# A fused attention and cosine-gated MLP kernel: the order of all engines and the sharing of copies and squares chosen anew

## The chip, the cores and the metric

The kernel runs on one core of one Trainium2 chip. The core has a matrix engine (TensorE, in the profile PE, with its weight loads as PEld), a vector engine (VectorE, DVE), an activation engine (ScalarE, ACT), a general engine (GpSimd, POOL) and a queue engine for transfers (SyncE, SP). The metric is device time in microseconds (us) of one execution, lower is better. The engines run side by side and wait for each other through semaphores.

## The reference

```python
q_n = q / (norm(q) + 1e-06); k_n = k / (norm(k) + 1e-06)      # 8 x 12 heads, 448 x 64
scores = q_n @ k_n.T / 0.1
attn = softmax(scores)                                          # over the last axis
x = (attn @ v), heads side by side                              # 3584 x 768
h = x @ w_in                                                    # 768 x 2048
out = (h * cos(h)) @ w_out                                      # 2048 x 768, float32
```

So there is cosine attention for 8 batches of 12 heads, and a gated two-layer MLP on all 3,584 tokens.

## The kernel before, in words

**Tiling.** Two heads make a "group" (48 groups, numbered g), three groups a "unit" (16 units u, half of a batch), six groups a batch b. For a unit, k and q are loaded (`load`), squared (`square`, label sq), summed over 64 columns (`reduce`, red), turned into reciprocal norms (`rnorm`) and scaled (`scale`). A scaled group is transposed (label T, or TP for the first nine, which TensorE transposes), and TensorE computes its scores in four pieces SC g.0 to SC g.3, where piece 0 is half as wide. ScalarE turns each piece into exponentials (exp g.c). From those TensorE forms the weighted values and the sums (`attend`: steps R, AV, S). VectorE can add exponentials in pairs first ("folds": fold g; "tails": tail g), so that TensorE has fewer sums to form: a group with two folds needs two matmul steps fewer than one with one fold, and a tail saves one R step.

**Normalising.** For groups that are not in the list `direct`, the unnormalised result is copied out of PSUM (label xu, by ScalarE if g is in the list `acts`, otherwise by VectorE, lines 1114 to 1117). Per unit, `chain` (line 1182) collects the sums by a transfer, takes reciprocals, writes them to memory and broadcasts them back into RB (labels gather, recip, spread, bcast). `multiply` (line 1170) then forms x g, on VectorE if g is in the list `fast`, otherwise on GpSimd. Both are line 1175.

**MLP.** For each batch b, M1 b.n computes sixteen blocks of 128 features (6 matmuls each over 448 tokens, line 1209), in eight pairs; ScalarE takes the cosine (sin, line 1240) and VectorE the product (g, line 1242). M1 b needs x of all six groups of its batch; `m1` in the plan says how many pairs begin with a part of the groups, from which group on they go singly, in which PSUM bank each pair stands, and in which order the groups are taken. M2 t computes 128 output rows (28 tiles t): as quarter-size matmuls (line 1309) or, from tile 21 on, as full ones (line 1338). A tile's two halves are copied out of PSUM by ScalarE if (t, half) is in `oacts` (line 1274) and otherwise by VectorE (line 1276), and stored.

**Order.** TensorE's order is written out in the plan ("order", some 1,450 entries, a label and a count each), and so is the bank of each step ("script"). The other engines' orders come from a planner in the kernel's own code (class `Program`, `arrange` and `play`, lines 367 to 563): it plays the program through with assumed costs, and at each moment lets an engine take, among what is ready, the operation with the earliest due time. The due time is counted back from TensorE's order, plus a number of its own for each operation (`bias`, some 1,000 numbers). The planner also plays the instruction packets of TensorE: 256 instructions each, where `ins` is the number of instructions that an operation holds. The result is a fixed program: each engine has a list of instructions in order and waits on semaphores. SyncE's list holds the loads, transposes, gathers, broadcasts and stores; GpSimd issues the loads of v and of the weights.

**Dummies.** At the start, while data is awaited, TensorE runs dummy matmuls on a zeroed buffer (line 1375).

Of the kernel before, what the change touches and what calls it, by code (L numbers as in the profile page):

```python
# [1595 lines left out]
```

## Time and profile before

| What | us |
|---|---|
| median of 3 runs | 419.7 |
| lowest, highest | 419.03, 424.96 |
| profiled execution, its own time | 419.64 |
| its span, first to last instruction | 417.7 |
| TensorE busy | 405.9 |
| ScalarE busy | 289.1 |
| VectorE busy | 242.6 |
| GpSimd busy | 217.8 |

The span is what the trace covers; 1.9 us of the execution's time lie around it. Busy time of TensorE is the union of its matmuls' records; consecutive matmuls overlap in the records, so the duration of one is longer than the time that it adds. In a row of groups stand the line, the engine, the operation, the output and inputs, the shape and the count, then busy time and mean duration in nanoseconds, then the idle time before them and what ended it. In rows in order of time the first number is the start, the second the length, and the bracket tells of idle time before and who ended it.

### The profile page before, as it was taken

The page shows a single profiled execution, that of the slowest core. Times are in us where ns is not written, and L with a number is a line of the kernel's source. Part 1 is how long each engine was busy: PE and PEld are TensorE (multiplying, and loading weights), DVE is VectorE, ACT ScalarE, POOL GpSimd, SP SyncE. Part 2 cuts the span into 40 slices and gives each one's busy share as a digit, 9 for nine tenths or more (in the row PEclk, how much of TensorE's full clock was granted, in tenths as well). Part 3 has the DMA queues.
Part 4 walks back from the last instruction along what each step waited for, and adds up shares of the span by engine and source line. Part 5 has one row for each costly group of instructions (what it writes and reads, how often), then busy time and mean ns, then how long its engine had stood idle before and what let it go on. Part 6 is the DMA issues. An engine that isn't in the chain of part 4 may idle for free.

```text
span 417.7 us, 14563 instructions
## 1 busy us (share of the span) xinstructions
PE 405.9 (97%) x6511; PEld 255.7 (61%) x6511; DVE 242.6 (58%) x321; ACT 289.1 (69%) x403; POOL 217.8 (52%) x173
## 2 busy tenths in 40 slices
...
PEclk9999999999999999999999999999999999999999
...
GB/s 190 251 258 221 206 213 182 173 151 197 197 118 146 170 236 186 101 140 219 236 92 87 192 269 83 137 198 215 206 81 96 186 3 3 105 123 2 5 72 113
DMA packets 77352, 63.31 MB, mean 152 GB/s; under 512 B 42090, under 2 KB 72298, under 8 KB 77290
## 3 DMA queue, kind: packets, MB, share of 16 engines
...
q0 software_dynamic: 18048, 12.59, 20.3%
q8 instruction: 51, 0.84, 0.8%
...
q10 hardware_dynamic: 160, 0.10, 0.1%
...
## 4 chain that ended last, share of the span: by engine, by line
PE 85%; ACT 4%; DVE 4%; DMA 3%; POOL 2%; issue 1%; SPq 0%; DVEq 0%; ACTq 0%; POOLq 0%
PE MP L1309 22%; PE SC L1209 21%; PE AV L1209 10%; PE MP L1338 5%; PE SC L975 5%; PE AV L1057 4%; PE MP L1209 4%; PE SC L1057 4%; PE SC L1338 3%; DMA RB<-scr 1%; ACT PX L989 1%; DMA scr<-rcp 1%; PE AV L975 1%; POOL qks L918 1%; PE SC L982 1%
## 5 line engine op out<-in xcount | busy, mean ns | idle before, releaser
L1309 PE MATMUL MP<-W,gT 64*64 64x384 bf16 x2688 | 137.3, 323 | 0.5 <-DVE qkT L956 0.4
L989 ACT ACTIVATE PX<-SC 128x896 bf16<-128x896 f32 x116 | 103.3, 917 | 13.5 <-PE SC L975 10.9
L1209 PE MATMUL SC<-xT,W 128*128 128x448 bf16 x468 | 96.9, 353 | 0.0
L1309 PEld LDWEIGHTS MP<-W,gT 64*64 64x64 bf16 x2688 | 80.9, 107 | 24.3 <-issue 2.3
L918 POOL TENSOR_TENSOR qks<-raw,rn 128x896 bf16<-128x896 f32 (+1 forms) x45 | 75.2, 1681 | 31.7 <-ACT rn L910 14.2
L1175 POOL TENSOR_TENSOR xT<-xu,RB 128x448 bf16<-128x448 f32 x39 | 44.4, 1151 | 84.4 <-DMA RB<-scr 42.9
L1209 PEld LDWEIGHTS SC<-xT,W 128*128 128x128 bf16 x468 | 45.4, 98 | 43.2 <-issue 1.5
L1240 ACT ACTIVATE cosb<-SC,cst 128x896 f32<-128x896 f32 x39 | 39.1, 1007 | 45.1 <-PE SC L1209 41.3
L1242 DVE TENSOR_TENSOR gT<-SC,cosb 128x896 bf16<-128x896 f32 x39 | 42.3, 1090 | 42.1 <-ACT cosb L1240 40.7
L887 DVE TENSOR_REDUCE n<-sq 128x14 f32<-128x896 bf16 (+2 forms) x49 | 51.0, 1057 | 12.4 <-ACT sq L878 8.8
L880 POOL TENSOR_TENSOR sq<-raw 128x896 bf16<-128x896 f32 x31 | 52.0, 1693 | 11.0 <-DVE n L887 5.8
L993 DVE TENSOR_TENSOR FO<-PX 128x896 bf16<-128x896 bf16 x37 | 30.0, 811 | 32.6 <-ACT PX L989 32.4
L1209 PE MATMUL AV<-xT,W 128*128 128x448 bf16 x216 | 48.1, 353 | 0.0
L975 PE MATMUL SC<-qkT 64*64 64x448 bf16 x464 | 42.4, 354 | 0.8 <-ACT PH L989 0.3
L854 POOL DMA_DIRECT2D va<-in_v_dram x32 | 21.9, 692 | 22.8 <-PE AV L1057 10.2
L1209 PEld LDWEIGHTS AV<-xT,W 128*128 128x128 bf16 x216 | 20.7, 98 | 19.6 <-issue 0.9
L1276 DVE COPY osb<-MP 128x384 f32<-128x384 f32 x38 | 20.1, 553 | 21.2 <-PE MP L1309 12.3
L989 ACT ACTIVATE PX<-AV 128x896 bf16<-128x896 f32 x28 | 25.7, 917 | 3.9 <-PE AV L975 3.8
L1240 ACT ACTIVATE cosb<-AV,cst 128x896 f32<-128x896 f32 x18 | 18.1, 1006 | 14.9 <-PE AV L1209 12.1
L1338 PE MATMUL MP<-W,gT 128*128 128x384 bf16 x128 | 24.9, 326 | 0.0
L1057 PE MATMUL AV<-PX,va 64*64 64x224 bf16 x480 | 23.1, 258 | 1.7 <-issue 1.3
L1242 DVE TENSOR_TENSOR gT<-AV,cosb 128x896 bf16<-128x896 f32 x18 | 19.6, 1087 | 8.6 <-ACT cosb L1240 7.1
...
## 6 DMA issues: line engine op xcount, KB each, us to landing
...
W<-in_moe_w_out_dram POOLq DMA_DIRECT2D x4, 768.0 KB, 19.3
...
```

The costliest lines, as they stand in the source:

```text
L880: pool(lambda e, x=x, y=y: e.tensor_tensor(y, x, x, ALU.mult), src_, dst, 0.1 + n * 1.78e-3, label="sq%d.%d" % (u, p)).pad = LATE if u > 1 ...
L887: dve(lambda e, w=w: e.tensor_reduce(out=n2v[i][:, 2 * p : 2 * p + 2, w], in_=sqv[p][:, :, w, :], axis=mybir.AxisListType.X, op=ALU.add), ...
L918: f = lambda e, s0=s0, s1=s1: e.tensor_tensor(qksv[i][:, p, s0:s1].rearrange("p s h d -> p h s d"), rawv[i][:, h, s0:s1, :], bass.AP(rn[i] ...
L975: m = e.matmul(ph[BP * o : BP * o + BP, a, 0:S], t[r, c - 1 + (NT3 + 1) * o, 0:BP], x, start=True, stop=True)
L989: act(lambda e: e.activation(PHv[g % 3] if c == 0 else PXv[j][:, c - 1], ph[:, :, 0:n], ACT.Exp, scale=1.0 / TAU), keys, [("PX", j, c) if ...
L1057: m = e.matmul(av_[64 * a : 64 * a + 64, b, x], w, source(kind, c)[r, a, SH * h : SH * h + SH], start=(h == 0 and c == 0 and kind == "V" a ...
L1175: f = lambda e: e.tensor_tensor(x, a, r, ALU.mult)
L1209: t = e.matmul(ph[:, a, 0:S], W1v[:, order[c], 128 * n : 128 * n + 128], xTv[b % 2][:, order[c], :], start=(c == 0), stop=(c == NKC - 1))
L1240: act(lambda e, ph=ph, cz=cz: e.activation(cosv[cz], ph[:, :, 0:S], ACT.Sin, bias=cst.ap()[:, 0:1], scale=1.0), names(gi) + ["cst0"], [("c ...
L1242: dve(lambda e, ph=ph, cz=cz, gi=gi: e.tensor_tensor(gTv[:, 2 * gi : 2 * gi + 2, S * (b % 2) : S * (b % 2) + S], ph[:, :, 0:S], cosv[cz], ...
L1309: r = e.matmul(POH[b][x : x + 64, 0:HW], gTv[k, y, col + x : col + x + 64], W2v[k, y, HW * b : HW * b + HW], start=(y == 0 and h == 0), st ...
L1338: r = e.matmul(po[:, 0 : w[1] - w[0]], gTv[:, y, col : col + 128], W2v[:, y, w[0] : w[1]], start=(y == 0), stop=(y == NF - 1))
```

## The change

Only lists in the plan change, and one number that the planner uses. The functions stay as they are.

- `acts`: which groups' results ScalarE copies out of PSUM.
- `oacts`: which output halves ScalarE copies; 17 before, 24 after.
- `folds`, `tails`: group 16 has two folds in place of one; 13 and 27 get a tail, 30 and 47 lose it; the entries for 8, 9 and 25 belong to groups without folds.
- `squared`, `scaled`: which squares of q and k ScalarE takes (14 before, 12 after; the rest GpSimd), and which three scalings VectorE takes.
- `fast`: which x VectorE multiplies; 3 before, 8 after.
- `m1` for batches 3, 4 and 5; `made`, `flat`.
- `order`, `script` and `bias`: nearly every line is new.
- `ins` of the step B (the spread of reciprocals in the first batch) is 8 in place of 4.

```diff
-    "acts": (7, 8, 9, 17, 18, 19, 22, 24, 25, 26, 28, 29, 30, 34, 35, 37, 40, 42, 43, 44, 47),
-    "oacts": ((0, 0), (4, 0), (5, 0), (10, 0), (12, 0), (13, 0), (14, 0), (16, 0), (16, 1), (21, 0), (22, 1), (23,
-        1), (25, 0), (25, 1), (26, 0), (26, 1), (27, 0)),
-    "made": {1: 4, 2: 8, 3: 11, 4: 13, 5: 27, 6: 20, 8: 21},
+    "acts": (10, 11, 18, 19, 22, 23, 26, 28, 29, 30, 34, 36, 37, 40, 43, 44, 45, 46, 47),
+    "oacts": ((0, 0), (2, 1), (4, 0), (5, 0), (6, 1), (9, 1), (10, 0), (13, 0), (14, 0), (16, 0), (16, 1), (18, 0),
+        (19, 1), (20, 0), (21, 1), (22, 0), (23, 0), (23, 1), (24, 0), (25, 0), (26, 0), (26, 1), (27, 0), (27, 1)),
+    "made": {1: 5, 2: 7, 3: 12, 4: 13, 5: 25, 6: 20, 8: 21},
     "fold": 2,
-    "folds": {6: 2, 7: 0, 8: 0, 9: 0, 10: 1, 11: 1, 12: 2, 13: 1, 14: 1, 15: 1, 16: 1, 17: 0, 18: 1, 21: 1, 25: 0},
+    "folds": {6: 2, 7: 0, 8: 0, 9: 0, 10: 1, 11: 1, 12: 2, 13: 1, 14: 1, 15: 1, 16: 2, 17: 0, 18: 1, 21: 1, 25: 0},
     "tailed": 1,
-    "tails": {6: 0, 7: 0, 8: 1, 9: 1, 10: 0, 11: 0, 12: 0, 13: 0, 14: 0, 15: 0, 16: 0, 17: 0, 18: 1, 21: 0, 27: 0,
-        28: 0, 33: 0, 35: 1, 39: 1, 40: 0, 42: 0, 43: 0},
+    "tails": {6: 0, 7: 0, 8: 0, 9: 0, 10: 0, 11: 0, 12: 0, 13: 1, 14: 0, 15: 0, 16: 0, 17: 0, 18: 1, 21: 0, 25: 0,
+        27: 1, 28: 0, 30: 0, 33: 0, 35: 1, 39: 1, 40: 0, 42: 0, 43: 0, 47: 0},
...
-    "scaled": {(2, 0): "D", (13, 1): "D", (15, 2): "D"},
-    "squared": {(3, 1): "A", (4, 1): "A", (5, 2): "A", (10, 0): "A", (10, 1): "A", (10, 2): "A", (11, 0): "A", (11,
-        1): "A", (12, 2): "A", (13, 0): "A", (13, 1): "A", (13, 2): "A", (14, 0): "A", (15, 1): "A"},
+    "scaled": {(3, 1): "D", (6, 1): "D", (15, 2): "D"},
+    "squared": {(3, 1): "A", (5, 2): "A", (8, 1): "A", (9, 0): "A", (9, 2): "A", (10, 0): "A", (10, 1): "A", (10,
+        2): "A", (11, 1): "A", (13, 0): "A", (15, 0): "A", (15, 1): "A"},
...
-        1, 4)), 3: (3, 2, (0, 2, 1, 0, 2, 1, 0, 2), (0, 1, 2, 5, 3, 4)), 4: (3, 2, (1, 0, 2, 3, 1, 0, 2, 1), (2, 1,
-        0, 3, 4, 5)), 5: (3, 5, (2, 1, 0, 3, 2, 1, 0, 2), (0, 1, 2, 3, 5, 4)), 6: (3, 3, (1, 0, 2, 3, 1, 0, 2, 1),
+        1, 4)), 3: (3, 2, (0, 2, 1, 0, 2, 1, 0, 2), (2, 5, 1, 0, 3, 4)), 4: (4, 2, (1, 0, 2, 3, 1, 0, 2, 1), (2, 1,
+        0, 3, 4, 5)), 5: (4, 5, (2, 1, 0, 3, 2, 1, 0, 2), (0, 1, 2, 3, 5, 4)), 6: (3, 3, (1, 0, 2, 3, 1, 0, 2, 1),
...
-    "flat": (),
-    "fast": (27, 33, 42),
+    "flat": (21,),
+    "fast": (21, 27, 30, 33, 34, 39, 42, 45),
...
-            w = P.op("PE", spread, ["sel0", "sel1", ("gT", 1, NF // 2 - 1), ("RB", i, p)], ["PO"], cost=0.76, mode="F", label="B%d" % g, ins=4)
+            w = P.op("PE", spread, ["sel0", "sel1", ("gT", 1, NF // 2 - 1), ("RB", i, p)], ["PO"], cost=0.76, mode="F", label="B%d" % g, ins=8)
```

The first line of the TensorE order, before and after, as a sample of the rest:

```diff
-        TP0*2 SC0.0 SC0.1 TP1 SC0.2 TP1 SC0.3 SC1.1 SC1.0 TP2 SC1.2 TP2 R0*2 SC2.0 AV0 S0*3 SC1.3 TP3*2 AV0*2 SC2.1 SC2.2
+        TP0*2 SC0.1 SC0.3 SC0.0 TP1*2 SC0.2 SC1.1 SC1.0 TP2*2 SC1.2 R0*2 AV0 S0*2 SC1.3 AV0*2 SC2.0 TP3 S0 SC2.1 SC2.2
...
```

The new order and biases were picked by playing the plan through with lateness drawn at random for transfers and instruction packets.

More of the change, by code (lines that the diff above doesn't have):

```diff
@@ new lines @@
+        TP0*2 SC0.1 SC0.3 SC0.0 TP1*2 SC0.2 SC1.1 SC1.0 TP2*2 SC1.2 R0*2 AV0 S0*2 SC1.3 AV0*2 SC2.0 TP3 S0 SC2.1 SC2.2
+        TP3 R1*2 AV1*2 S1*2 AV1 S1 B0 SC2.3 SC3.0 R2*2 S2 AV2 S2 AV2*2 S2 SC3.1 SC3.2 B1 SC3.3 R3 TP4*2 R3 AV3*3 S3*3
+        SC4.0 SC4.1 B2 R4 SC4.2 TP5*2 SC4.3 B3 SC5.0 R4 SC5.1 AV4 S4*3 AV4*2 SC5.2 SC5.3 M1_0.0 M1_0.1 M1_0.0 R5 M1_0.2
+        R5 AV5 S5*2 AV5*2 S5 M1_0.3 M1_0.4 M1_0.5 M1_0.1 M1_0.0 M1_0.4 M1_0.1 M1_0.6 M1_0.5 M1_0.2 M1_0.3 M1_0.7 M1_0.8
+        M1_0.9 M1_0.10 M1_0.12 M1_0.13 TP6*2 M1_0.11 M1_0.14 TP7*2 M1_0.15 TP8*2 SC6.0 SC6.1 M2_0*4 SC6.2 M2_0 R6*2 AV6
@@ new lines @@
+        SC6.3 SC7.0 M2_0*3 AV6*2 SC7.2 AV6 SC7.1 M2_0*2 SC8.0 AV6*4 SC7.3 M2_0*2 SC8.2 M2_0*2 SC8.1 M2_0 R7*2 AV7 M2_0
+        AV7*6 SC8.3 AV7 M2_1 AV7*3 M2_1*2 AV7 SC9.0 M2_1 SC9.1 M2_1*3 AV8*6 R8*2 SC9.3 SC9.2 AV8*5 M2_1 SC10.1 AV8 M2_1*3
+        SC10.0 M2_1*3 SC10.2 M2_1*2 SC10.3 R9*2 AV9*6 SC11.0 AV9*4 SC11.1 AV9*2 M2_2*3 SC11.2 SC11.3 M2_2*4 R10*2 AV10
+        M2_2 AV10*4 M2_2 SC12.0 AV10*5 M2_2*3 SC12.1 M2_2*4 AV11*5 R11*2 SC12.2 SC12.3 AV11*5 M1_1.0 M1_1.1 M1_1.2 M1_1.3
+        M1_1.2 M1_1.6 M1_1.7 M1_1.6 M1_1.7 M1_1.0 M1_1.1 M1_1.0 M1_1.1 M1_1.0 M1_1.6 M1_1.7 M1_1.6 M1_1.3 M1_1.2 M1_1.3
@@ new lines @@
+        M1_1.2 M1_1.3 M1_1.7 M1_1.6 M1_1.7 M1_1.2 M1_1.3 M1_1.1 M1_1.4 M1_1.0 M1_1.1 M1_1.5 M1_1.4 M1_1.5 M1_1.4 M1_1.5
+        M1_1.4 M1_1.5 M1_1.4 M1_1.5 M1_1.8 M1_1.9 M1_1.12 M1_1.13 M1_1.10 M1_1.11 M1_1.14 M1_1.15 R12*2 AV12*4 SC13.0
+        AV12*3 M2_3*3 AV12 SC13.1 M2_3*2 SC13.2 M2_3 SC13.3 M2_3*2 R13 AV13 M2_3 SC14.0 M2_3 AV13*4 SC14.1 AV13*3 SC14.2
+        AV13*2 M2_3*2 SC14.3 M2_3*2 SC15.0 M2_3*2 SC15.1 R14*2 AV14*5 SC15.2 AV14*5 SC15.3 M2_4*2 SC16.0 M2_4*2 R15
+        SC16.1 R15 M2_4 AV15 SC16.2 M2_4 AV15*4 SC16.3 M2_4 AV15*3 SC17.0 AV15*2 M2_4 SC17.1 M2_4*2 SC17.2 M2_4 AV16
@@ new lines @@
+        SC17.3 AV16*3 R16*2 M2_4 AV16*4 M2_4 SC18.0 M2_4*3 AV17 SC18.1 AV17*5 R17*2 SC18.2 M2_5 AV17 M2_5 AV17 SC18.3
+        AV17*4 R18 M2_5*2 SC19.0 AV18 M2_5*4 SC19.2 M2_5 SC19.1 M2_5 AV18*2 M2_5*2 SC20.0 M2_5*4 AV18*2 SC20.1 AV18*5
+        M2_6 SC19.3 M2_6*7 R19 AV19 SC20.3 M2_6 AV19*2 SC20.2 AV19 M2_6*2 SC21.1 AV19*3 M2_6 AV20*2 AV19 M2_6*2 SC21.2
+        M2_6 SC21.0 AV20*2 R20 M2_6 AV20*3 SC21.3 AV20 M1_2.2 M1_2.3 M1_2.2 M1_2.6 M1_2.7 M1_2.0 M1_2.3 M1_2.2 M1_2.3
+        M1_2.2 M1_2.3 M1_2.2 M1_2.4 M1_2.1 M1_2.0 M1_2.6 M1_2.7 M1_2.1 M1_2.0 M1_2.1 M1_2.0 M1_2.3 M1_2.6 M1_2.7 M1_2.5
@@ new lines @@
+        M1_2.4 M1_2.5 M1_2.4 M1_2.5 M1_2.1 M1_2.0 M1_2.1 M1_2.6 M1_2.4 M1_2.7 M1_2.6 M1_2.7 M1_2.5 M1_2.4 M1_2.5 M1_2.8
+        M1_2.9 M1_2.10 M1_2.11 M1_2.12 M1_2.14 M1_2.13 M1_2.15 M2_7*3 AV21*3 M2_7*2 AV21*2 R21*2 SC22.1 M2_7*2 AV21*3
+        SC22.0 AV21*2 M2_7 SC22.2 M2_7*2 SC22.3 M2_7 SC23.0 M2_7*3 SC23.1 M2_7*2 SC23.2 AV22*4 R22 SC23.3 AV22*4 M2_8*4
+        SC24.1 SC24.0 R23 AV23*2 M2_8*3 SC24.2 AV23 M2_8 AV23 SC24.3 M2_8 AV23*4 M2_8*2 SC25.1 M2_8*5 AV24*2 SC25.0
+        AV24*2 R24 SC25.3 AV24*4 SC25.2 M2_9*4 SC26.0 SC26.1 SC26.2 M2_9*4 AV25 SC26.3 M2_9 AV25*4 SC27.0 AV25 R25*2 M2_9
@@ new lines @@
+        AV25*2 AV26 M2_9*2 AV25*4 AV26*3 R26 SC27.1 M2_9 AV26*4 M2_9*3 SC27.3 SC27.2 M1_3.0 M1_3.1 M1_3.0 M1_3.1 M1_3.0
+        M1_3.1 M1_3.0 M1_3.2 M1_3.3 M1_3.2 M1_3.1 M1_3.0 M1_3.1 M1_3.3 M1_3.2 M1_3.4 M1_3.5 M1_3.4 M1_3.5 M1_3.4 M1_3.5
+        M1_3.3 M1_3.2 M1_3.3 M1_3.2 M1_3.4 M1_3.5 M1_3.4 M1_3.3 M1_3.5 M1_3.6 M1_3.7 M1_3.8 M1_3.9 M1_3.10 M1_3.11
+        M1_3.12 M1_3.13 M1_3.14 M1_3.15 M2_10 R27 M2_10 AV27*4 M2_10 AV27*4 M2_10 SC28.0 SC28.1 M2_10*3 SC28.3 M2_10
+        SC28.2 M2_10*2 SC29.2 SC29.0 M2_10*2 SC29.1 M2_10*4 AV28*4 R28 SC29.3 SC30.0 R28 M2_11*2 AV28*4 R29 AV29*3 M2_11
@@ new lines @@
+        SC30.1 M2_11 AV29 SC30.2 AV29*4 M2_11*4 SC30.3 M2_11*4 SC31.1 M2_11*4 AV30*3 SC31.0 AV30 R30*2 SC31.2 AV30*4
+        SC31.3 M2_12*4 SC32.1 M2_12 SC32.0 M2_12*2 SC32.2 AV31*3 M2_12 AV31 R31 M2_12 AV31*4 SC32.3 SC33.1 M2_12*5 SC33.0
+        M2_12*2 SC33.2 SC33.3 M1_4.0 M1_4.1 M1_4.0 M1_4.1 M1_4.2 M1_4.3 M1_4.6 M1_4.4 M1_4.5 M1_4.4 M1_4.5 M1_4.2 M1_4.3
+        M1_4.4 M1_4.0 M1_4.5 M1_4.2 M1_4.3 M1_4.2 M1_4.3 M1_4.4 M1_4.1 M1_4.0 M1_4.1 M1_4.5 M1_4.0 M1_4.1 M1_4.4 M1_4.5
+        M1_4.2 M1_4.3 M1_4.7 M1_4.6 M1_4.7 M1_4.6 M1_4.7 M1_4.6 M1_4.7 M1_4.6 M1_4.7 M1_4.8 M1_4.10 M1_4.9 M1_4.11
@@ new lines @@
+        M1_4.12 M1_4.13 M1_4.14 M1_4.15 R32 AV32*3 R33 AV32 R33 AV33 AV32 AV33 AV32*3 AV33*2 M2_13 AV33*4 M2_13*3 SC34.0
+        M2_13 SC34.1 M2_13*3 SC34.2 M2_13 SC34.3 M2_13*5 SC35.1 M2_13*2 R34 AV34*2 SC35.0 AV34*2 SC35.3 AV34*4 M2_14*6
+        SC36.0 SC35.2 M2_14*2 SC36.1 M2_14*5 SC36.3 M2_14 AV35*3 M2_14*2 AV35 R35 SC37.2 SC36.2 AV35*4 M2_15*4 SC37.0
+        M2_15*4 SC37.1 M2_15 SC37.3 M2_15*2 R36 AV36*4 M2_15 AV36*4 M2_15*4 AV37 SC38.0 AV37*3 R37 SC38.2 AV37*4 SC38.1
+        M2_16*5 SC38.3 M2_16*3 SC39.1 SC39.0 M2_16*3 SC39.2 M2_16 R38 AV38 M2_16*3 AV38*3 M2_16 SC39.3 AV38*4 M1_5.0
@@ new lines @@
+        M1_5.1 M1_5.0 M1_5.1 M1_5.2 M1_5.3 M1_5.2 M1_5.3 M1_5.4 M1_5.5 M1_5.4 M1_5.6 M1_5.8 M1_5.9 M1_5.5 M1_5.7 M1_5.6
+        M1_5.7 M1_5.10 M1_5.11 M1_5.12 M1_5.13 M1_5.14 M1_5.15 M2_17*2 R39 AV39*3 M2_17 AV39 M2_17 AV39*4 SC40.0 M2_17*2
+        SC40.1 M2_17*2 SC40.2 M2_17 SC41.0 M2_17*2 SC40.3 M2_17 SC41.1 M2_17*2 SC41.2 M2_17*2 SC41.3 R40*2 AV40*4 SC42.0
+        AV40*3 M2_18 AV40 M2_18*2 R41 AV41 SC42.1 AV41*3 SC42.2 AV41*4 M2_18 SC42.3 M2_18*3 SC43.0 AV42 M2_18 SC43.1 AV42
+        M2_18*2 SC43.2 M2_18 SC43.3 AV42*2 M2_18*2 R42*2 AV43 M2_18 AV43 SC44.0 M2_18*2 AV43*2 R43*2 AV42*4 SC44.1
@@ new lines @@
+        M2_19*4 SC44.3 M2_19*2 SC44.2 AV43*4 M2_19*2 SC45.2 M2_19 SC45.0 M2_19*5 SC45.1 SC45.3 M2_19*2 M1_6.2 M1_6.4
+        M1_6.5 M1_6.0 M1_6.3 M1_6.1 M1_6.4 M1_6.2 M1_6.3 M1_6.0 M1_6.1 M1_6.5 M1_6.4 M1_6.2 M1_6.3 M1_6.5 M1_6.0 M1_6.1
+        M1_6.4 M1_6.0 M1_6.1 M1_6.5 M1_6.6 M1_6.7 M1_6.2 M1_6.3 M1_6.8 M1_6.9 M1_6.12 M1_6.10 M1_6.13 M1_6.11 M1_6.14
+        M1_6.15 M2_20 AV45*3 AV44*4 R44 AV45 R45 AV44*2 M2_20 AV44*2 M2_20 SC46.0 AV45*4 M2_20*3 SC46.2 M2_20*2 SC46.1
+        SC46.3 M2_20 SC47.1 M2_20*4 AV46*2 M2_20*3 SC47.0 AV46*2 R46 SC47.3 AV46*4 SC47.2 M2_22*5 M2_21*2 M2_22*2 M2_21*2
@@ new lines @@
+        R47*2 AV47*8 M2_21*6 M2_22 M2_21*6 M2_22*4 M2_23*5 M2_22*4 M2_23*2 M1_7.0 M1_7.1 M1_7.2 M1_7.3 M1_7.0 M1_7.1
+        M1_7.2 M1_7.3 M2_23 M1_7.2 M1_7.4 M1_7.5 M1_7.4 M1_7.3 M1_7.2 M1_7.3 M1_7.2 M1_7.5 M1_7.4 M1_7.3 M1_7.5 M1_7.4
+        M1_7.0 M1_7.1 M1_7.0 M1_7.1 M1_7.5 M1_7.0 M1_7.1 M2_23*2 M1_7.4 M1_7.5 M1_7.8 M2_23 M2_24*2 M1_7.6 M1_7.7 M1_7.10
+        M1_7.11 M2_23*2 M1_7.12 M1_7.9 M2_25 M2_23*3 M1_7.13 M2_24*3 M1_7.14 M1_7.15 M2_24*3 M2_25 M2_24 M2_26 M2_24*2
+        M2_26*4 M2_25*3 M2_26 M2_24*5 M2_25*2 M2_26*2 M2_27*2 M2_26 M2_27 M2_26*2 M2_27 M2_26 M2_25*8 M2_26 M2_25 M2_26*3
@@ L267 @@
+        M2_27*20
         """,
     "script": """
-        s6.0=2 s6.1=1 s6.2=2 s6.3=1 a6=0 s7.0=2 s7.1=1 d6=0 c6=0 s7.2=2 s7.3=1 s8.0=2 d7=0 s8.1=1 a7=0 s8.2=2 s8.3=2 c7=0
-        s9.0=2 d8=0 s9.1=1 s9.2=2 a8=0 s9.3=1 c8=0 s10.0=2 s10.1=1 s10.2=2 a9=0 d9=0 c9=0 s10.3=1 s11.0=2 a10=0 s11.1=1
-        s11.2=2 s11.3=1 d10=0 c10=0 s12.0=2 s12.1=1 d11=0 a11=0 s12.2=2 s12.3=1 c11=0 m1 a12=0 s13.0=2 s13.1=1 d12=0
-        c12=0 s13.2=2 a13=0 s13.3=1 s14.0=2 s14.1=1 d13=0 c13=0 s14.2=2 a14=0 s14.3=1 s15.0=2 s15.1=1 s15.2=2 d14=0 c14=0
@@ L283 @@
[L283 to L287 removed]
+        s6.0=2 a6=0 s6.1=1 s6.2=2 s6.3=1 s7.0=2 s7.1=1 d6=0 c6=0 s7.2=2 s7.3=1 a7=0 s8.0=2 d7=0 s8.1=1 c7=0 s8.2=2 s8.3=2
@@ new lines @@
+        s9.0=2 d8=0 s9.1=1 a8=0 s9.2=2 s9.3=1 s10.0=2 c8=0 s10.1=1 s10.2=2 s10.3=1 a9=0 d9=0 c9=0 s11.0=2 s11.1=1 s11.2=2
+        s11.3=1 a10=0 d10=0 c10=0 s12.0=2 s12.1=1 d11=0 s12.2=2 s12.3=1 a11=0 c11=0 m1 a12=0 s13.0=2 s13.1=1 d12=0 c12=0
+        s13.2=2 a13=0 s13.3=1 s14.0=2 s14.1=1 d13=0 c13=0 s14.2=2 s14.3=1 s15.0=2 s15.1=1 a14=0 d14=0 s15.2=2 c14=0
+        s15.3=1 s16.0=2 s16.1=1 a15=0 d15=0 s16.2=2 c15=0 s16.3=1 s17.0=2 s17.1=1 s17.2=2 d16=0 a16=0 s17.3=1 c16=0
+        s18.0=2 d17=0 a17=0 s18.1=1 s18.2=2 s18.3=1 s19.0=1 c17=0 s19.1=0 s19.2=1 a18=2 s19.3=0 a19=0 d19=0 s20.0=1 d18=2
```

82 lines of the change are left out of this document (13 added, 69 removed), and 282 rows, old and new, of the table PLAN.

## The prediction

> **What bounds the kernel now.** I read the page's busy shares first, then the busy time by stage, then the waits of TensorE, then the single places where it stands.
>
> ```profile
> span 417.7 us, 14563 instructions
> PE 405.9 (97%) x6511; PEld 255.7 (61%) x6511; DVE 242.6 (58%) x321; ACT 289.1 (69%) x403; POOL 217.8 (52%) x173
> PEclk9999999999999999999999999999999999999999
> ...
> q8 instruction: 51, 0.84, 0.8%
> ```
>
> TensorE is recorded busy for 97% of the span at full clock; no other engine passes 69%. So the end moves only by TensorE's own work or by the time it stands. The stages (length, then PE, weight loads, DVE, ACT, POOL):
>
> ```profile
> core 0: us, PE busy (x) PEld busy (x) DVE busy (x) ACT busy (x) POOL busy (x), PEclk, DMA share, GB/s
> 0.00:12.00 12.00, 10.03 (x50) 4.44 (x50) 5.22 (x15) 6.09 (x12) 6.59 (x14) 1.00 0.87 198
> 12.00:20.00 8.00, 6.69 (x88) 2.97 (x86) 3.09 (x5) 7.11 (x13) 7.85 (x6) 1.00 1.21 255
> 20.00:28.00 8.00, 7.59 (x117) 3.94 (x111) 5.08 (x8) 7.40 (x16) 7.91 (x7) 1.00 1.19 247
> ...
> 36.00:57.00 21.00, 20.93 (x154) 10.87 (x152) 16.28 (x17) 12.78 (x16) 19.48 (x15) 1.00 1.22 208
> 57.00:88.00 31.00, 29.44 (x780) 21.37 (x772) 15.09 (x25) 28.94 (x48) 20.54 (x13) 1.00 0.93 189
> ...
> 106.00:147.00 41.00, 39.27 (x1066) 31.04 (x1063) 25.79 (x35) 33.92 (x49) 24.28 (x19) 1.00 0.89 156
> ...
> 253.00:286.00 33.00, 32.21 (x849) 23.73 (x851) 22.96 (x33) 25.61 (x37) 17.17 (x14) 1.00 0.85 149
> ...
> 371.00:396.00 25.00, 25.00 (x143) 13.52 (x140) 7.64 (x8) 9.29 (x11) 3.32 (x3) 1.00 0.08 28
> 396.00:418.00 22.00, 18.39 (x129) 11.95 (x127) 3.56 (x5) 5.41 (x9) 0.00 (x0) 0.97 0.34 90
> sum 418.00, PE 405.92 PEld 255.69 DVE 242.56 ACT 289.15 POOL 217.80; mean PE 20.30 PEld 12.78 DVE 12.13 ACT 14.46 POOL 10.89
> ```
>
> TensorE stands 418.00 - 405.92 = 12.1 us in all. The first three windows hold 1.97 + 1.31 + 0.41 = 3.7, the last one 3.6 (the last copy and store). What is left, 12.1 - 3.7 - 3.6 = 4.8 us, lies in the 368 us between, and three stages hold nearly all of it: 1.56 (57 to 88), 1.73 (106 to 147), 0.79 (253 to 286). **That is the prize: 4.8 us of visible waiting, 1.1%.** 2% would be 8.4 us. Some of the start is hidden behind dummy matmuls, but there POOL is busy 15.76 of 16 us (12 to 28), on squares and scalings of the first two units that the change leaves where they are; I give the start nothing, with 1 us to either side.
>
> Two of the three places are single events:
>
> ```profile
> 137.78 0.29 PE L1057 MATMUL AV<-PX,va 64*64 64x224 bf16 x3
> 139.37 0.28 PE L1057 MATMUL AV<-PX,va 64*64 64x224 bf16 x1 [1.31 <-issue]
> ```
>
> TensorE stops for 1.31 us between the third and fourth matmul of one group, waiting for no engine. I read it as a late instruction packet: 51 packets came on the instruction queue (page above), for 13,022 weight loads and matmuls, one per 256. This is the only stop of that kind of this size.
>
> ```profile
> 282.40 0.63 DVE L1175 TENSOR_TENSOR xT<-xu,RB 128x448 bf16<-128x448 f32 x1 [3.78 <-DMA RB<-scr]
> ...
> 283.70 1.57 POOL L1175 TENSOR_TENSOR xT<-xu,RB 128x448 bf16<-128x448 f32 x1 [2.33 <-DVE FO L993]
> ...
> 284.32 1.20 DVE L998 TENSOR_TENSOR FO<-FO,PH 128x448 bf16<-128x448 bf16 x1
> ...
> 285.58 0.29 PE L1057 MATMUL AV<-FO,ones 64*64 64x224 bf16 x4 [0.79 <-DVE FO L998]
> ```
>
> VectorE holds still for 3.78 us at x33 until the broadcast reciprocals land; then x34 on GpSimd runs 283.70 to 285.27, and the fold beside it takes 1.20 us. TensorE loses 0.79 us.
>
> **The change, part by part.** Durations by engine and line (count, busy us, mean ns, then idle before and its cause):
>
> ```profile
> L1274 ACT ACTIVATE osb<-MP 128x384 f32<-128x384 f32 x12 | 5.9, 491 | 12.9 <-PE MP L1338 10.8 <-PE MP L1309 2.0
> L1276 DVE COPY osb<-MP 128x384 f32<-128x384 f32 x38 | 20.1, 553 | 21.2 <-PE MP L1309 12.3 <-PE MP L1338 7.8 <-PE AV L982 1.0
> L878 ACT ACTIVATE sq<-raw 128x896 bf16<-128x896 f32 x16 | 15.1, 945 | 0.4 <-DMA raw<-in_q_dram 0.4
> L880 POOL TENSOR_TENSOR sq<-raw 128x896 bf16<-128x896 f32 x31 | 52.0, 1693 | 11.0 <-DVE n L887 5.8 <-DMA raw<-in_q_dram 3.6 <-DVE FO L993 1.6
> L1175 DVE TENSOR_TENSOR xT<-xu,RB 128x448 bf16<-128x448 f32 x3 | 1.9, 620 | 3.8 <-DMA RB<-scr 3.8
> L1175 POOL TENSOR_TENSOR xT<-xu,RB 128x448 bf16<-128x448 f32 x39 | 44.4, 1151 | 84.4 <-DMA RB<-scr 42.9 <-DVE FO L998 23.5 <-DVE xT L1175 6.8
> L993 DVE TENSOR_TENSOR FO<-FO,PX 128x896 bf16<-128x896 bf16 x29 | 21.1, 729 | 4.1 <-ACT PX L989 2.7
> L998 DVE TENSOR_TENSOR FO<-FO,PH 128x448 bf16<-128x448 bf16 x22 | 9.4, 429 | 0.8
> ```
>
> *TensorE's work.* Counting the entries of the two written orders: the only label whose number of matmuls changes in sum is AV16, two groups fewer, since group 16 gets a second fold. Four "tails" change and cancel (13 and 27 lose an R step, 30 and 47 gain one; 8, 9 and 25 have no fold and so no tail). The finer steps of M1 4 and 5 split the same matmuls. "flat" for tile 21 and the new "made" numbers select nothing that differs, and the 8 in place of 4 at the reciprocal spreads only tells the planner how many instructions they are; none is added.
>
> ```profile
> 286.20 0.29 PE AV L1057 x12
> ```
>
> Twelve such matmuls take 0.29 us on the chain, so a group of four 0.096: two groups are **-0.2 us**. Changes between array shapes go from 54 to 55: nothing.
>
> *Engine loads.* "oacts" gains eleven output copies and drops four: ScalarE +7 x 0.491 = +3.4, VectorE -7 x 0.553 = -3.9. Of "acts" only groups that are not "direct" count: 36, 45, 46 come, 24, 25, 42 go, 15 before and after: nothing. "squared" goes from 14 to 12: ScalarE -2 x 0.945 = -1.9, GpSimd +2 x 1.693 = +3.4. "fast" goes from 3 to 8: VectorE +5 x 0.620 = +3.1, GpSimd -5 x 1.151 = -5.8. "scaled" keeps three, at other places. Fold 16 adds 0.73 to VectorE; the tails there cancel. In sum ScalarE +1.5, VectorE about 0, GpSimd -2.4 us over 418: no engine nears TensorE, so **0**, covered by TensorE's 97%. Where the cover fails is locally, from 57 to 88, where ScalarE is busy 28.94 of 31 us.
>
> *The queues.* The new biases sort all five engines' lists, SyncE's transfers and GpSimd's among them: as many loads, transposes and stores as before, in another sequence. A late load shows first in the squares: GpSimd's stood 3.6 us for loads (row above) with no cost on TensorE. **0**, bounds 0 and +3.6, all of that passed on.
>
> *The order, 57 to 88 us.* Walking both written orders at the trace's pitches, I compared, at each of 291 reuses of a PSUM bank, TensorE's time between last write and next write with the reader's mean duration. Before, three fall short (by 0.31, 0.25 and 0.12 us), the first two in this stage; after, two (0.12 and 0.06). I take **-0.4 us**; bounds -1.56 (all of the stage's idle) and +0.5 (the new order meets other waits).
>
> *The stop at 138.* Another order puts other instructions at the packets' edges. One packet in 51 was late here; nothing says that the next order has none. Bounds -1.31 and +1.31 (a second one); I take half of the gain, **-0.6**. The Trainium skill's "Runtime: NRT & Kernel Launch", section "Instruction fetch mechanics", says that the sequencer prefetches 256-instruction blocks and that a crossing is mostly hidden. The trace agrees for 50 of 51; by the page the planned-for lateness has nearly nothing to win.
>
> *x34 and x33 at 283.* Both go to VectorE (x30 too), so no GpSimd multiply runs beside the fold: **-0.8**, bounds -0.8 and 0 (the late broadcast alone could still cost it). The Trainium skill's "Perfetto Trace Analysis", section "Optimizing Scalar/DVE Operations", says that the two engines share a read port and that moving work between them might not help. The fold's 1.20 us against its mean of 0.429 agrees with the port; by the page the five moves are worth 0.
>
> *Waits that are added.* Seven of the eight multiplies on VectorE that matter (x21, x27, x30, x33, x39, x42, x45) are the first of their unit, so a VectorE instruction now waits for a broadcast at four more units. Behind it on VectorE are folds, output copies and gating products, for which TensorE waits. Before, one of three waited, 3.78 us, and TensorE lost 0.79: some 3.0 us are covered. Eight places at one in three are 2.7 such waits against one: +1.7 x 0.79 = +1.3; bounds 0 and +5.5 (eight of 0.79, less the one). x34 is second in its unit and waits little. I take **+0.8**, nearer the low end, since two of three waited not at all.
>
> Sum: -0.2 - 0.4 - 0.6 - 0.8 + 0.8 = -1.2 us. The profiled execution took 419.64 (span 417.7 and 1.9 around it), the median is 419.7: **418.4 us**.
>
> **The rivals.**
>
> *The waiting really goes.* The whole 4.8 us between start and end, 0.2 of work and up to 1 at the start: 413.6 us. For it: three named places hold 4.1 of it and two are addressed. Against: about 1,450 order entries are all rearranged; each has new neighbours.
>
> *VectorE held by broadcasts.* One mechanism on the slow side: the first multiply of units 7, 9, 10, 11, 13, 14, 15 sits on VectorE until its reciprocals land. It decides once a wait passes the 3.0 us of cover; beyond, each microsecond is TensorE's. At 3.78 in all eight: +5.5, 425.2; without x34 at half of the others +2, 421.6. To pass 2% the eight must average 3.0 + 8.4/8 = 4.0 us. For it: the 3.78 row. Against: GpSimd took such waits before (42.9 us in four, row above) without cost to TensorE, and VectorE is idle 42% of the time.
>
> *The change doesn't do what it says.* If lateness is hidden anyway and the order is as good as the old one, only the work's 0.2 stays, and new small waits replace old: 419.5 us. For it: TensorE's work is the same and the two events repaid are chance events. Against: x34 no longer runs beside the fold. The two pages of the Trainium skill named above point to this case.
>
> **How the numbers follow.** Forecast 418.4 (416.5 to 419.3): 0.40. No effect, 419.5 (up to 420.5): 0.23. Waiting gone, 413.6 (up to 416.5): 0.14. VectorE held, 421 to 425: 0.23, of which 0.05 beyond 428. The three runs span 419.03 to 424.96, 1.4%, so 2% is about what a measurement can tell. Range 413.6 to 425.2; half of the third case and a third of the fourth lie outside, about 0.15. Faster by over 2% (below 411.3) needs more than all visible waiting: 0.02. Slower by over 2% (above 428.1): 0.05. Within: 0.93.
>
> **What would show it.** Dummies aside, TensorE has 8 matmuls fewer. No 0.79 us wait for L998; VectorE's L1175 group at x8, GpSimd's at x34; the idle of the VectorE group below 7 us if I am right, 25 or more if the slow rival is. Stops put to "issue": one or none above 1 us. Stage 57 to 88 busy over 29.6. What would make me wrong: a start later by over 1 us, since nothing in the diff's lists moves it but the order does, or two or more late packets.

## The result and the profile after

The changed kernel takes 417.56 us (median of 20 runs, 416.00 to 420.14). The kernel before, run beside it 20 times, takes 420.57 (418.91 to 425.74). The ratio is 0.9927, with a 95% interval of 0.9906 to 0.9949: 3.0 us less, clear of no change, and far from 2%. On a second chip the changed kernel gave 0.9918 (0.9890 to 0.9945).

The page of the changed kernel's profile:

```profile
span 418.0 us, 14555 instructions
PE 405.0 (97%) x6502; PEld 253.2 (61%) x6502; DVE 242.6 (58%) x321; ACT 291.2 (70%) x409; POOL 215.3 (52%) x170
```

The engines' busy times are as before within 2.5 us. This execution took 420.14 us, the longest of the 20. Its waits of TensorE (who waited for whom, us in total, times, longest) show most of the reason:

```profile
PE AV L1060 <- issue: 2.3, 1, 2.3
PE MP L1378 <- DVE osb L1377: 1.9, 1, 1.9
PE MP L945 <- POOL qks L921: 1.4, 3, 0.7
PE MP L1312 <- issue: 0.8, 2, 0.6
PE SC L978 <- issue: 0.7, 1, 0.7
```

Three rows put to "issue" hold 3.8 us, where the profile before had 1.5 in two stops (1.31 and 0.23). Their length differs from execution to execution: another one of the same program, profiled on the second chip, has a span of 414.2 and these waits:

```profile
PE MP L1378 <- DVE osb L1377: 1.9, 1, 1.9
PE AV L1060 <- issue: 1.0, 1, 1.0
PE MP L1312 <- issue: 0.8, 2, 0.6
PE MP L945 <- POOL qks L921: 0.4, 1, 0.4
```

Their places return. In this second profile the three stops are

```profile
72.35 0.39 PE L1060 MATMUL AV<-PX,ones 64*64 64x224 bf16 x8 [0.95 <-issue]
...
78.01 0.48 PE L1312 MATMUL MP<-W,gT 64*64 64x384 bf16 x5 [0.57 <-issue]
...
83.03 0.68 PE L1312 MATMUL MP<-W,gT 64*64 64x384 bf16 x10 [0.25 <-issue]
```

and from each of them to the next some 255 matmuls and weight loads are recorded. The row from the first stop to the second (length, then PE, weight loads, DVE, ACT, POOL with their counts):

```profile
72.34:78.00 5.66, 4.96 (x127) 3.73 (x128) 1.68 (x3) 4.39 (x7) 5.66 (x3) 1.00 1.12 169
```

So the stops stand one packet of 256 instructions apart, at places that the program fixes, and the runs further down with the new order have them before the same matmuls (us; a dash where no wait put to "issue" is listed there):

| before the matmul group | first profile | second | five multiplies back | output copies back | squares back | all lists back | added traffic | loads cut |
|---|---|---|---|---|---|---|---|---|
| AV with ones, x8 or x9 | 2.31 | 0.95 | 0.67 | 0.41 | 2.31 | - | 2.31 | - |
| M2, x5 | 0.57 | 0.57 | 0.57 | 0.85 | - | - | 2.22 | - |
| M2, x10 | 0.25 | 0.25 | 0.53 | 0.25 | - | 0.51 | 1.07 | - |

Stops near 68 and 192 us (0.20 to 0.68) come in some of them as well. The same holds for the old order: its stop of 1.31 us at 139 us returns, before the same matmul, in all four other profiles of that order (0.64 to 1.13).

Below I compare with the second profile. To see where the 3.5 us between the spans go, take the first matmul of an M1 stage (start, length, line, count) as a milestone: batches 0, 1, 2 and 5, first before,

```profile
35.25 0.93 PE L1209 MATMUL MP<-xT,W 128*128 128x448 bf16 x4
...
88.66 1.12 PE L1209 MATMUL MP<-xT,W 128*128 128x448 bf16 x5
...
147.13 1.12 PE L1209 MATMUL AV<-xT,W 128*128 128x448 bf16 x5
...
286.70 1.12 PE L1209 MATMUL SC<-xT,W 128*128 128x448 bf16 x5
```

then in the changed kernel, second profile:

```profile
34.15 1.12 PE L1212 MATMUL MP<-xT,W 128*128 128x448 bf16 x5
...
89.59 0.93 PE L1212 MATMUL MP<-xT,W 128*128 128x448 bf16 x4
...
145.78 1.12 PE L1212 MATMUL AV<-xT,W 128*128 128x448 bf16 x5
...
283.52 1.12 PE L1212 MATMUL SC<-xT,W 128*128 128x448 bf16 x5
```

The opening is 1.1 us shorter. From M1 0 to M1 1 it loses 2.0 (55.44 against 53.41), of which 1.8 are the three stops above. From M1 1 to M1 2 it wins 2.3, of which 1.5 are the two stops that the profile before had there. From there to M1 5 it wins 1.8 (3.2 in all by then), and 0.3 more to the end. So no single wait carries the gain.

The groups of the moved work, VectorE's x, GpSimd's x, ScalarE's output copies in the first profile after:

```profile
L1178 DVE TENSOR_TENSOR xT<-xu,RB 128x448 bf16<-128x448 f32 x8 | 5.8, 727 | 3.9 <-DMA RB<-scr 3.9
...
L1178 POOL TENSOR_TENSOR xT<-xu,RB 128x448 bf16<-128x448 f32 x34 | 38.7, 1150 | 72.2 <-ACT RB L1128 29.0 <-DVE xT L1178 21.3 <-DVE FO L1001 11.2
...
L1277 ACT ACTIVATE osb<-MP 128x384 f32<-128x384 f32 x21 | 10.3, 490 | 20.1 <-PE MP L1341 17.1 <-PE MP L1312 1.9 <-DVE osb L1279 1.0
```

VectorE waits 3.9 us in sum for broadcasts at eight multiplies, against 3.8 at three.

### The profile page after: what moved, and what is told of

The parts are those of the page before. It is cut to its first block, busy times and chain, and to the rows that moved or that the text cites. A ratio compares the mean times of both kernels' runs of the same rounds, so it can differ in the third digit from the quotient of the medians.

```text
span 418.0 us, 14555 instructions
## 1 busy us (share of the span) xinstructions
PE 405.0 (97%) x6502; PEld 253.2 (61%) x6502; DVE 242.6 (58%) x321; ACT 291.2 (70%) x409; POOL 215.3 (52%) x170
## 4 chain that ended last, share of the span: by engine, by line
PE 88%; ACT 3%; POOL 3%; DMA 2%; issue 2%; DVE 1%; SPq 1%; ACTq 0%; DVEq 0%; POOLq 0%
PE MP L1312 24%; PE SC L1212 21%; PE AV L1212 9%; PE SC L978 5%; PE MP L1341 5%; PE AV L1060 4%; PE SC L1060 4%; PE MP L1212 4%; PE SC L1341 3%; DMA RB<-scr 1%; PE AV L978 1%; ACT PX L992 1%; POOL qks L921 1%; PE AV L1042 1%; DMA raw<-in_q_dram 1%
## 5 line engine op out<-in xcount | busy, mean ns | idle before, releaser
L992 ACT ACTIVATE PX<-SC 128x896 bf16<-128x896 f32 x114 | 100.6, 917 | 14.1 <-PE SC L978 13.3
L1312 PEld LDWEIGHTS MP<-W,gT 64*64 64x64 bf16 x2688 | 79.6, 107 | 27.5 <-issue 4.6
L1178 POOL TENSOR_TENSOR xT<-xu,RB 128x448 bf16<-128x448 f32 x34 | 38.7, 1150 | 72.2 <-ACT RB L1128 29.0
L883 POOL TENSOR_TENSOR sq<-raw 128x896 bf16<-128x896 f32 x33 | 55.3, 1683 | 30.2 <-DMA raw<-in_q_dram 15.2
L996 DVE TENSOR_TENSOR FO<-PX 128x896 bf16<-128x896 bf16 x37 | 31.8, 859 | 35.6 <-ACT PX L992 35.2
L978 PE MATMUL SC<-qkT 64*64 64x448 bf16 x456 | 40.8, 353 | 1.9 <-issue 0.7
L992 ACT ACTIVATE PX<-AV 128x896 bf16<-128x896 f32 x30 | 27.6, 920 | 2.0 <-PE AV L978 1.8
L1279 DVE COPY osb<-MP 128x384 f32<-128x384 f32 x29 | 15.4, 555 | 17.7 <-PE MP L1312 12.4
L1277 ACT ACTIVATE osb<-MP 128x384 f32<-128x384 f32 x21 | 10.3, 490 | 20.1 <-PE MP L1341 17.1
L992 ACT ACTIVATE PH<-SC 128x448 bf16<-128x448 f32 x37 | 20.2, 545 | 5.4 <-PE SC L985 5.0
```

Source lines behind the costliest of these rows:

```text
L883: pool(lambda e, x=x, y=y: e.tensor_tensor(y, x, x, ALU.mult), src_, dst, 0.1 + n * 1.78e-3, label="sq%d.%d" % (u, p)).pad = LATE if u > 1 ...
L978: m = e.matmul(ph[BP * o : BP * o + BP, a, 0:S], t[r, c - 1 + (NT3 + 1) * o, 0:BP], x, start=True, stop=True)
L992: act(lambda e: e.activation(PHv[g % 3] if c == 0 else PXv[j][:, c - 1], ph[:, :, 0:n], ACT.Exp, scale=1.0 / TAU), keys, [("PX", j, c) if ...
L1178: f = lambda e: e.tensor_tensor(x, a, r, ALU.mult)
L1312: r = e.matmul(POH[b][x : x + 64, 0:HW], gTv[k, y, col + x : col + x + 64], W2v[k, y, HW * b : HW * b + HW], start=(y == 0 and h == 0), st ...
```

## The experiments

Two theories stood at first: the gain lies in the order (O) or in the sharing of work (S). A second pair: the gain is the order's own (O) or comes from bearing late transfers (L). In the kernels called "places kept", the plan is made with the original lists, and each operation keeps its place in time when it is given to another engine. That isolates the sharing, but an operation that is given back gets a place that was found for another engine's duration; so these numbers are upper bounds of what the sharing is worth, or of the harm that it does. No run let the planner order the other engines anew for the changed lists. The runs stand on three chips; each has the kernel before beside it, and ratios are to that.

### The changed kernel beside the others

No edit.

> The changed kernel as it is, so that the runs beside it have it on the same chip. Both theories: 0.993 of the kernel before, that is 2.5 to 3.5 us less, with stops put to "issue" between 0.3 and 4 us in sum, as the packets fall.

Measured: 416.78 us against 419.91, ratio 0.9918, as expected.

### Loads cut: is the gain the order's own?

```diff
+        rows = BP if u < 4 else 8
...
-            rawv[i][BP * x : BP * x + BP, h].rearrange("p h s d -> p h (s d)"), src(t, u, 2 * p0, 2 * (p1 - p0)))
+            rawv[i][BP * x : BP * x + rows, h].rearrange("p h s d -> p h (s d)"), src(t, u, 2 * p0, 2 * (p1 - p0), rows))
...
```

(the same for v), in the kernel before and in the changed one.

> The kernel before with the loads of q, k and v from unit 4 on cut to 8 of 64 rows (the rest of the buffers keeps older units, so the output is not the reference's); same instructions, same places. If the changed kernel's gain is that it bears late transfers and packets (theory L): this one comes down by about 3 us, to 416 to 417, and its scatter shrinks. If the gain lies in the order by itself (theory O): it comes down by 0.5 to 1.5 us, the stops put to "issue" alone.

> The changed kernel with the same cut of the loads. Theory L: it hardly moves and meets the cut kernel before within 0.7 us. Theory O: it also comes down by 0.5 to 1.5 us and stays 2 to 3 us below the cut kernel before.

Measured: 417.65 us (417.15 to 419.01) and 414.39 (413.99 to 414.97), against 419.45 for the kernel before: ratios 0.9942 (0.9910 to 0.9973) and 0.9859 (0.9803 to 0.9915). Both come down by about 2 us, more than theory O named and less than theory L named for the kernel before. The difference between them, 3.3 us, is as large as with all loads, and this decides for theory O: late loads of q, k and v in ordinary runs don't carry the gain. The cut changed kernel is the only one whose waits have no "issue" row of 0.2 us or more:

```profile
PE MP L1380 <- DVE osb L1379: 1.9, 1, 1.9
PE SC L980 <- ACT xu L1120: 0.4, 1, 0.4
```

The cut kernel before still has some:

```profile
PE AV L1059 <- issue: 0.7, 1, 0.7
PE MP L1311 <- issue: 0.5, 1, 0.5
```

So in the changed kernel the three stops of the table are gone with the loads; in the kernel before they are about as large as in its ordinary profile (1.2 us in sum against 1.5). That fewer loads make the stops shorter is seen in one profile of the two, no more.

### Loads made later

```diff
+            if PLAN.get("junk") and u >= 4:
+                f.append(lambda e: e.dma_start(
+                    bass.AP(junk, (UP * u + p0) * 2 * BP * NB * D, [[2 * NB * D, BP], [NB * D, 2], [1, NB * D]]), src(k, u, 2 * p0, 2)))
+                x = (0, 1, 2)
...
```

> The kernel before with each load from unit 4 on followed by a third transfer of the same size from memory to memory, for which the load's semaphore also waits; places kept. Theory L: the lateness costs it clearly more than the changed kernel, 5 us or more. Theory O: both lose alike, within 2 us.

> The changed kernel with the same added transfers. Theory L: it loses at most half of what the kernel before loses. Theory O: it loses the same within 2 us and stays 2 to 4 us below.

Measured: 433.67 and 426.86 us, ratios 1.0322 (1.0243 to 1.0400) and 1.0156 (1.0085 to 1.0226) to the kernel before. The kernel before loses 3.2%, the changed one 2.4% (1.0156 less the 0.9918 above, from other runs): 14 and 10 us. That lies between the theories, neither half nor the same. Whether the changed kernel bears great lateness better is not shown: with four runs each, the losses are 2.4 to 4.0% and, by the same subtraction, 1.7 to 3.1%, and these overlap. Besides, the four runs of the kernel before had a lower mean granted clock (0.984 to 0.995) than those of the changed one (0.995 to 1.000); by an estimate from these means, about 0.007 of 430 us, that alone is some 3 of the 4 us. In both, stops put to "issue" now hold more in sum; the longest is 3.0 us, where ordinary runs have up to 2.31. The kernel before:

```profile
PE SC L1014 <- issue: 3.0, 1, 3.0
PE MP L1341 <- issue: 2.8, 3, 2.4
```

and the changed one:

```profile
PE MP L1344 <- issue: 3.3, 2, 2.2
PE AV L1092 <- issue: 2.8, 2, 2.3
```

### The sharing taken back, and the sharing alone

Five lists (`acts`, `oacts`, `squared`, `scaled`, `fast`) as before in the changed kernel, and as after in the kernel before, places kept.

```diff
+SHARED = dict(PLAN)
+SHARED.update({
+    "acts": (7, 8, 9, 17, 18, 19, 22, 24, 25, 26, 28, 29, 30, 34, 35, 37, 40, 42, 43, 44, 47),
...
+    "fast": (27, 33, 42),
+})
```

> The changed kernel with the old sharing (copies, squares, scalings and multiplies on the engines that had them before), every operation at the place in time that the new plan gives it. If the order makes the gain (theory O): within 1.2 us of the changed kernel, so 1.5 to 3.5 us under the kernel before. If the sharing makes it (theory S): the gain is gone, within 1 us of the kernel before.

> The kernel before with the new sharing, places in time kept. Theory O: within 1 us of the kernel before. Theory S: 2 to 3 us less.

Measured: the new order with the old sharing takes 420.54 us, ratio 1.0004 (0.9979 to 1.0030): the gain is gone, as theory S has it. But the old order with the new sharing takes 425.92 in four runs, ratio 1.0145 (1.0073 to 1.0217): slower by 1.5%, which neither theory had. Its mean granted clocks are 0.991 to 0.999, but the run at 0.999 took 424.0 us as well. Both theories fall in their simple form: order and sharing fit each other, and with the places kept each without the other gives nothing or harm.

### The sharing in three parts

The same, with one list or two at a time.

> The changed kernel with only the five multiplies given back to GpSimd (x21, x30, x34, x39, x45), places kept. If VectorE is held by broadcasts: up to 1.3 us less than the changed kernel. If the port between VectorE and GpSimd is what counts: 0.5 to 1 us more, with a fold beside a multiply that takes 1.2 us. If neither reaches TensorE: the same within 0.5 us.

> The changed kernel with only the output copies shared as before, places kept. The old sharing as a whole cost 3.8 us against the changed kernel, the multiplies alone 0.8 of it. If the output copies carry the rest (VectorE busy with them when a fold or an output is due): 419 to 420 us. If they don't: 417 us, within 0.7 of the changed kernel.

> The changed kernel with only the squares and scalings shared as before, places kept. If these carry the rest: 418.5 to 420 us, most of it lost where units 3, 6 and 8 to 14 are prepared. If not: 417 us, within 0.7 of the changed kernel.

Measured, as ratios to the kernel before, where the changed kernel has 0.9918:

| given back | us | ratio (interval) | lost |
|---|---|---|---|
| five multiplies | 417.58 | 0.9941 (0.9915 to 0.9966) | 0.23% |
| output copies | 418.52 | 0.9973 (0.9947 to 0.9999) | 0.55% |
| squares and scalings | 417.95 | 0.9943 (0.9916 to 0.9970) | 0.25% |
| all five lists | 420.54 | 1.0004 (0.9979 to 1.0030) | 0.86% |

By the medians the output copies carry most. The interval of the output copies begins where that of the changed kernel ends (0.9947 and 0.9945); the two small ones are not told apart from the changed kernel, nor the three parts from each other. The output copies alone (expected 419 to 420, or 417) and the squares and scalings (expected 418.5 to 420, or 417) came out between their expectations. The multiplies cost 0.8 us against the changed kernel on the same chip, which is what the case of the port named, but its sign is missing: the tail folds take 0.429 us on average in both. The result copies (`acts`) were not given back alone. For the output copies the profile shows one place where they cost: the last tile before an M1 stage. With the old output copies, both halves of tile 6 are copied by VectorE, with other work between them, and the first M1 matmul in that bank waits (line order: copy, copy, weight load, matmul):

```profile
145.74 0.56 DVE L1307 COPY osb<-MP 128x384 f32<-128x384 f32 x1 [1.17 <-PE MP L1340]
...
147.25 0.55 DVE L1307 COPY osb<-MP 128x384 f32<-128x384 f32 x1
...
147.86 0.93 PE L1240 MATMUL MP<-xT,W 128*128 128x448 bf16 x4 [0.61 <-DVE osb L1307]
```

In the changed kernel ScalarE takes the second half when VectorE is done with the first, and the matmul has no wait:

```profile
145.40 0.56 DVE L1279 COPY osb<-MP 128x384 f32<-128x384 f32 x1 [1.22 <-PE MP L1312]
...
146.04 0.49 ACT L1277 ACTIVATE osb<-MP 128x384 f32<-128x384 f32 x1 [0.45 <-DVE osb L1279]
...
146.74 0.92 PE L1212 MATMUL MP<-xT,W 128*128 128x448 bf16 x4
```

The time between the start of the first copy and the matmul is 2.12 us with the old copies and 1.34 with the new. In the whole of that kernel the waits of this kind come to 1.2 us in two places:

```profile
PE MP L1240 <- DVE osb L1307: 1.2, 2, 0.6
```

The profile with all five lists given back has the same two waits, 1.2 us in sum. That is half of what the output copies cost when given back (0.55% is 2.3 us); the other half has no row of its own.

The kernel before has the old copies too, with the same work of VectorE between them, and no such wait. Its order takes that bank only as the third of M1 2, after the second copy has ended:

```profile
146.73 0.56 DVE L1276 COPY osb<-MP 128x384 f32<-128x384 f32 x1 [0.36 <-PE MP L1309]
...
148.20 0.55 DVE L1276 COPY osb<-MP 128x384 f32<-128x384 f32 x1
...
149.03 1.30 PE L1209 MATMUL MP<-xT,W 128*128 128x448 bf16 x6
```

With the new sharing in the old order it is ScalarE's copy that comes too late for this bank. It stands at the place kept from VectorE's second copy, and ScalarE has exponentials and a table load of 1.28 us ahead of it:

```profile
148.15 1.28 ACT L835 ACT_TABLE_LOAD   x1
...
149.44 0.49 ACT L1307 ACTIVATE osb<-MP 128x384 f32<-128x384 f32 x1
...
149.99 1.31 PE L1242 MATMUL MP<-xT,W 128*128 128x448 bf16 x6 [0.80 <-ACT osb L1307]
```

So these waits tell why the new order needs its own sharing, and in part why the old order is harmed by it. They are not a part of the gain over the kernel before, which has neither.

### One multiply moved in the kernel before

```diff
+SHARED = dict(PLAN)
+SHARED.update({
+    "fast": (27, 33, 34, 42),
+})
...
```

> The kernel before with one operation moved: x34 from GpSimd to VectorE, place kept. If the port held by x34 makes the stop at 285 us (my step): the 0.79 us wait for the tail fold is gone and the time 0.5 to 0.9 us less. If the late broadcast makes it: the wait stays, the time is the same.

Measured: 420.26 us, ratio 0.9978 (0.9943 to 1.0014): not told apart from no change. At its place, VectorE's x33, x34 and the tail fold, then TensorE:

```profile
284.54 0.62 DVE L1202 TENSOR_TENSOR xT<-xu,RB 128x448 bf16<-128x448 f32 x1 [2.92 <-DMA RB<-scr]
285.62 0.62 DVE L1202 TENSOR_TENSOR xT<-xu,RB 128x448 bf16<-128x448 f32 x1
...
286.81 0.39 DVE L1025 TENSOR_TENSOR FO<-FO,PH 128x448 bf16<-128x448 bf16 x1
...
287.62 0.27 PE L1084 MATMUL AV<-FO,ones 64*64 64x224 bf16 x4
```

The fold takes 0.39 us in place of 1.20, and TensorE's wait of 0.79 is gone. But VectorE waited 2.92 us for the broadcast here, not 3.78, and so the run does not part the two causes. The kernel before with the loads cut has x34 on GpSimd and a fold as slow as ever; its broadcast came sooner too, and TensorE has no wait there either:

```profile
280.31 0.63 DVE L1177 TENSOR_TENSOR xT<-xu,RB 128x448 bf16<-128x448 f32 x1 [2.79 <-DMA RB<-scr]
...
282.23 1.21 DVE L1000 TENSOR_TENSOR FO<-FO,PH 128x448 bf16<-128x448 bf16 x1
...
283.52 0.27 PE L1059 MATMUL AV<-FO,ones 64*64 64x224 bf16 x4
```

So a slow fold alone does not make the stop; as far as these profiles show, a late broadcast is needed with it. Nearest to a test of the move is the old order with the new sharing: its VectorE waited 3.61 us at x33, the fold took 0.39 and TensorE did not wait, but five lists had moved there. The ten times lie in two bunches, four of 417.7 to 418.1 and six of 419.4 to 422.2, so the interval is too wide for 0.8 us; the profiled one belongs to the upper bunch (below).

### The new opening alone

The kernel before with the changed kernel's order up to the last transpose TP8, on all engines, and two scalings shared as there:

```diff
+        cut = max(o.start for o in opening.ops if o.label == "TP8")
...
+            if (o.label, n) in early:
+                o.start, o.end = early[o.label, n].start, early[o.label, n].end
```

> The kernel before with the changed kernel's order of all engines up to the end of the first batch's M1 (some 55 us), and the old order from there on. If a third of the gain is made in the opening: M1 of batch 0 begins at 34.2 us and not at 35.2, and the time is 0.7 to 1.2 us less than before. If the rest makes all of it: the same as before within 0.4 us.

Measured: 418.85 us against 419.75, ratio 0.9965 (0.9935 to 0.9995). The median is 0.9 us less, the ratio of the runs 1.5 (0.2 to 2.7): by the medians the opening makes a third of the gain, by the ratio nearly half, and the interval allows from less than a tenth to nine tenths. In its profile M1 0 begins at 34.15, as expected. But M1 1 begins at 88.67, where the kernel before had it at 88.66, with 0.66 us in a stop put to "issue" in between; so the profile does not show that the lead is kept.

## Why the prediction was right, point by point, and where not

The forecast was 418.4, the range 413.6 to 425.2; the time is 417.56, within the range and to the side that was forecast. The size was too small: 1.2 us forecast, 3.0 measured (of this, 0.9 is that the kernel before has a median of 420.57 over 20 runs and had 419.7 over three). The 12.1 us for which TensorE stands count 0.3 us behind the end of the span (417.7, not 418.0); the 4.8 us of the prize are not touched by it. That the time lies within the range was in part luck. The range is 11.6 us wide, and most of the sum's terms were not borne out, while the opening and the fit of order and sharing, which the sum put at nothing, were worth something. What makes the rest of the gain stays open.

- *TensorE's work, -0.2:* held in number; the time was not tested by itself. 6,502 matmuls after 6,511, eight for group 16 and one dummy.
- *Engine loads, 0:* **this is the step that failed.** The sums were right (ScalarE +2.1 for +1.5 forecast, VectorE 0, GpSimd -2.5 for -2.4). But "covered by TensorE's 97%" looked at the stage from 57 to 88 alone, and left out who reads a bank last before an M1 stage. Given back in the new order, the lists cost up to 0.86%, the output copies 0.55% of it, and in M1 1 and M1 2 TensorE then waits 1.2 us for VectorE's copies. Moved work was not free; its price hung on the order beside it.
- *The start, nothing, with 1 us to either side:* mis-sized. It gave 1.1 us in the second profile and 0.9 in the run with the new opening alone. M1 0 starts at 34.1 to 34.8 us in the nine profiles with the new opening, and at 35.2 to 35.3 in four of the five with the old (the fifth is below). GpSimd was busy for 15.6 of the 16 us from 12 to 28 after the change too; that it is busy did not mean that TensorE's steps around it were in the best order.
- *The queues, 0:* held as far as tested: with the loads cut, the difference between the kernels stays (3.3 us).
- *The order from 57 to 88 us, -0.4:* not seen in ordinary runs. M1 1 starts 0.9 us later than before in the profile compared, and the three stops explain 1.8 of the 2.0 that were lost; without them the stage would be about as long as before. With the loads cut, where the changed kernel has no such stops, TensorE is busy for 0.6 us more of this stage than in the other kernel (kernel before, then changed); that is one profile of each:

```profile
57.00:88.00 31.00, 29.52 (x784) 21.29 (x780) 15.29 (x25) 28.90 (x48) 20.58 (x13) 1.00 0.57 101
...
57.00:88.00 31.00, 30.14 (x797) 21.77 (x798) 14.44 (x24) 28.33 (x49) 23.25 (x15) 1.00 0.60 116
```

- *The stop at 138, -0.6:* wrong. The stop is gone there, and others came: 1.8 us in one profile, 3.8 in the other. It was not one late packet of 51 either, since the profile before has a second stop, of 0.23 us. Nor was it the chance event that the third rival called it: the old order has it at this place in all five profiles, and the new order has three places of its own between 72 and 86 us. That it is a matter of the instruction packets is borne out by the 255 instructions between neighbouring stops; what makes one stop longer than another is open. By the Trainium skill's "Runtime: NRT & Kernel Launch", section "Instruction fetch mechanics", such crossings are mostly hidden. That agrees with most of the 51 packets and with the cut changed kernel, and not with the single stops of 2.31 us in an ordinary run and of 3.0 with added traffic.
- *x34 at 283, -0.8:* half right, and mis-sized. That the fold is slow beside GpSimd's multiply holds (1.20 and 1.21 us beside it, 0.39 without). But the stop was taken for a fixed cost, and it comes only with a late broadcast: of the four profiles with x34 on GpSimd in this order, the one before has it (0.79) and the one with added traffic (0.81), the one with the loads cut and the one with the new opening do not. The run that moves x34 alone had an early broadcast and could not test it.
- *Waits added, +0.8:* nothing seen, possibly the other sign. VectorE waited 3.9 us in sum at the eight, and giving the five multiplies back costs 0.23%, within the error. The rule that moves between GpSimd and VectorE might not help ("Perfetto Trace Analysis", section "Optimizing Scalar/DVE Operations", in the Trainium skill) is not borne out by that median, nor refuted.

The rivals: VectorE held by broadcasts is out (3.9 us of idle, no wait of TensorE above 0.2 us behind it). "No effect" is out (the interval ends at 0.9949). "The waiting really goes" named 413.6; the changed kernel reaches 416.0 in its best run, and 414.0 with the loads cut.

Of the signs named beforehand, the missing 0.79 us wait, the counts at line 1175 (now 1178) and VectorE's short idle came as said. Stage 57 to 88 did not: TensorE is busy for 26.65 us of it in the first profile, not over 29.6.

The change was drawn against lateness; whether it bears added traffic better is not shown, as said above. Whether the smaller scatter of the 20 runs (4.1 us against 6.8) comes from that is open.
